# Five dK tiles of a decode backward pass, each stored by two DMAs split along the partitions

## Chip, cores and metric

The kernel runs on one core of a Trainium2 chip. The metric is the device time of one execution in microseconds. The times of before are 742.79, 740.97 and 742.65 us, median 742.65 us.

## What is computed

One token passes through a layer norm and then, side by side, a decode attention block over a cache of 8192 positions (32 heads of 128) and a gated MLP. The reference returns the output and the gradients of all inputs but one:

```python
xn = layernorm(x)
q = (xn @ wq) as 32 heads
p = softmax(q . k_cache * 128 ** -0.5)
out = x + (p . v_cache) @ wo + (silu(xn @ w1) * (xn @ w3)) @ w2
return out, and the gradients of x, k_cache, v_cache, wq, wo, w1, w3, w2 for grad_out
```

All tensors are bf16. `k_cache`, `v_cache` and their gradients dK and dV are 64 MB each (32 heads x 8192 x 128). For one head, dV is the outer product of the probabilities p with the head's gradient `do`, and dK that of the score gradients U with the scaled query `qs`. So the kernel reads some 150 MB and writes as much, and most of it is K, V, dK and dV.

## The kernel before

**Tiles.** A head's 8192 positions lie on 128 partitions, 64 positions on each. A K or V tile is 128 x 64 x 128 bf16, 2 MB, one row of 16 KB on each partition, and this row is contiguous in memory as well. K and V are loaded by SyncE's queue (`load_k` L109, `load_v` L115), three K and two V buffers. dK and dV of a head are built in a tile `ot` of the same shape; the pool has four such buffers.

**Loop.** The main loop runs over the heads. In step h it does the score product of head h+1 (DVE multiplies, L365; TensorE adds up along the head dimension, L367), the softmax, the two attention sums (L429 and L451), and the two outer products of head h. `outer` is called four times in a step: for dV and dK, first and second half. In each half, ScalarE writes 8 of the 32 positions of a partition (L380) and VectorE the other 24 (L387). After the second half (`elif half:` in `outer_v`) the whole tile is stored by one DMA on GpSimd's queue (L394), and up to two pending column stores of a weight gradient follow (L396; these are there around heads 8 and 16 only). The last two heads (`TAIL`) are stored by SyncE's queue in halves (L392).

**What orders the work.** Each engine's instructions run in the order in which they are written. A buffer of `ot` is written again four tiles later, that is dK of head h uses the buffer of dK of head h-2, and its first writers on ScalarE and VectorE wait until the store of that earlier tile has landed. Loads are issued by SyncE as soon as the buffer's last reader is done.

**Queues.** In the profile, q0 is the queue of GpSimd's DMAs (software_dynamic), q1 that of SyncE and q10 that of ScalarE (hardware_dynamic). All of them run on the same 16 DMA engines. At the end of the kernel come the last column stores of wq's and wo's gradients, and the two small outputs, `dx_bf` (128 partitions x 5) by SyncE at L759 and `fin_bf` (5 partitions x 128) by ScalarE at L764.

**Names of the change.** `rows` is the view of `ot` as 128 partitions x 64 positions x 128, `dkc` and `dvc` are dK and dV in memory, seen as head, partition, position, element; `dst` is one of the two.

Of the kernel before, what the change touches and what calls it, by code (L numbers as in the profile page):

```python
# [16 lines left out]
P = 128  # L17
# [4 lines left out]
def kernel(  # L22
# [22 lines left out]
    nc = tc.nc  # L45
# [38 lines left out]
    dkc = out_2.rearrange("b h (p j) d -> (b h) p j d", p=P)  # L84
# [13 lines left out]
    with tc.manual_schedule(engines=ORDERED):  # L98
# [271 lines left out]
        def outer(st, vec, w2, wf, dst, h, half):  # L370
            outer_v(st, vec, w2, dst, h, half, outer_s(st, vec, wf, half))
# [12 lines left out]
        def outer_v(st, vec, w2, dst, h, half, j1):  # L384
            j0 = half * JH
            n = j1 - j0
            nc.vector.tensor_tensor(st.ot[:, j0:j1],  # L387
                                    vec.rearrange("p (a b) -> p a b", b=2).unsqueeze(1).to_broadcast([P, n, DH // 2, 2]),
                                    w2[:, j0:j1, :].unsqueeze(2).to_broadcast([P, n, DH // 2, 2]), ALU.mult)
            rows = st.ot[:].rearrange("p j a b -> p j (a b)")  # L390
            if h >= H - TAIL:
                nc.sync.dma_start(dst[h][:, j0:j0 + JH, :], rows[:, j0:j0 + JH, :])  # L392
            elif half:
                nc.gpsimd.dma_start(dst[h], rows)  # L394
                for _ in range(2 if len(columns) > 2 else len(columns)):
                    nc.gpsimd.dma_start(*columns.pop(0))  # L396

        columns = []

        def row_max(st):  # L400
            st.S = small.tile([P, J], F32, name="S_sb", bufs=1)
            nc.vector.tensor_reduce(st.S[:], st.ps["S"][:], AX.X, ALU.add)  # L402
            mrow = small.tile([P, 1], F32, name="mrow")
            nc.vector.tensor_reduce(mrow[:], st.S[:], AX.X, ALU.max)  # L404
            st.sm = ps_s.tile([P, 512], F32, name="sm", tag="sm")
            nc.tensor.matmul(st.sm[:, 8:8 + P], lhsT=mrow[:].to_broadcast([P, P]), rhs=ident_f[:], start=True, stop=True,  # L406
                             skip_group_check=True)
# [387 lines left out]
```

## Time and profile before

| | |
|---|---|
| time of the profiled execution | 739.76 us |
| its span, first to last instruction | 737.9 us |
| granted TensorE clock, mean | 0.774 |
| data moved | 303.69 MB, mean 412 GB/s |
| HBM read, written | 151.34 MB, 151.34 MB |
| stores of `ot` by GpSimd's queue (L394) | 60, of 2048 KB, landing after 30.5 us (median) |
| shortest and longest landing of an `ot` store | 15.2 us, 40.3 us |
| loads of K and V | 32 and 32, landing after 26.7 and 21.5 us (median) |
| idle time of DVE at L387 for an `ot` store to land | 28.2 us in 14 waits |
| idle time of DVE at L365 for a K load | 29.1 us in 16 waits |

A landing time runs from the issue of a DMA to the arrival of its last byte, queueing included. In the rows of the page, the busy share is that of the span; in the rows of stages, the columns are the stage, its length, the busy time of PE, PEld, DVE, ACT and POOL with the number of instructions, the granted clock, the mean busy share of the 16 DMA engines, and GB/s. In the chain in order of time, each row is a start, a length, and what ran or was waited for.

### The profile page before, as it was taken

Reading aid. Unit: us, or ns where it says so; the run is one execution under the profiler, and the core shown is the slowest. Engines: PE = TensorE matmul, PEld = TensorE weight load, DVE = VectorE, ACT = ScalarE, POOL = GpSimd, SP = SyncE. Lnnn points to the kernel's source line nnn. Section 1 sums busy time; section 2 is a strip of 40 time slices with the busy share of each in tenths; the row PEclk is TensorE's granted clock in tenths of the full one; section 3 lists DMA queues with packets and bytes.
Section 4 is the critical chain, followed back from the end, with each engine's and each line's share of the span. In section 5 each row is a group of like instructions: output and inputs, shape, how many; then the busy total and the mean of one; then the engine's idle time right before and its main releaser. Section 6 shows DMA issues by size and latency. Waiting matters only on the chain.

```text
span 737.9 us, 15773 instructions
## 1 busy us (share of the span) xinstructions
PE 560.1 (76%) x6498; PEld 326.3 (44%) x6513; DVE 628.8 (85%) x708; ACT 467.3 (63%) x1395; POOL 48.6 (7%) x93
## 2 busy tenths in 40 slices
PE   4768888786888788767788877787878767887860
PEld 3554445443544445434444434444444434454440
DVE  3689999997899989877998979699599988999990
ACT  2384566784678666674677656587377846777650
POOL 0010000000000110100000100100000000000100
PEclk9798779767777779667986788688678878867765
DMA  9998999999999999999999999999999999999992
GB/s 332 415 410 311 407 432 428 428 428 429 428 429 429 422 432 426 430 425 427 432 428 426 431 428 425 428 428 426 427 422 410 428 422 432 409 430 430 419 407 106
DMA packets 28389, 303.69 MB, mean 412 GB/s; under 512 B 3116, under 2 KB 4846, under 8 KB 10910
## 3 DMA queue, kind: packets, MB, share of 16 engines
q1 hardware_dynamic: 15202, 155.41, 50.6%
q0 software_dynamic: 11376, 139.42, 44.6%
q10 hardware_dynamic: 1740, 7.87, 2.6%
q8 instruction: 51, 0.84, 0.4%
q14 instruction: 20, 0.16, 0.1%
HBM read 151.34 MB, written 151.34 MB: 410 GB/s over the span
## 4 chain that ended last, share of the span: by engine, by line
DMA 60%; DVE 23%; PE 10%; ACT 3%; issue 1%; SPq 1%; DVEq 0%; ACTq 0%
DMA out_dram<-ot 33%; DMA Kt<-in_A_k_cache_dram 23%; DVE T L365 10%; DVE ot L387 8%; PE psS L367 3%; DMA out_dram<-wo_g 2%; DMA w3t<-in_B_w_dram 2%; ACT ot L380 2%; PE ob L451 1%; PE ob L429 1%; PE psDP L367 1%; DVE DP_sb L436 1%; SPq L158 1%; PE dx_ps L592 1%; DVE S_sb L402 1%
## 5 line engine op out<-in xcount | busy, mean ns | idle before, releaser
L367 PE MATMUL psDP<-T,ident_bf 128*128 128x512 bf16 x512 | 187.7, 533 | 58.0 <-DVE T L365 57.8
L367 PEld LDWEIGHTS <-ident_bf 128*128 128x128 bf16 x1024 | 123.8, 123 | 238.6 <-issue 191.1
L380 ACT ACTIVATE ot<-qs_g,Uf 128x128 bf16<-128x128 bf16 x496 | 151.5, 390 | 60.4 <-DMA out_dram<-ot 18.3
L365 DVE TENSOR_TENSOR T<-Kt,qs_g 128x4096 bf16<-128x4096 bf16 x64 | 146.4, 2289 | 30.6 <-DMA Kt<-in_A_k_cache_dram 29.1
L367 PE MATMUL psS<-T,ident_bf 128*128 128x512 bf16 x512 | 152.2, 451 | 21.6 <-DVE T L365 21.4
L380 ACT ACTIVATE ot<-do_g,Pf 128x128 bf16<-128x128 bf16 x504 | 154.0, 389 | 5.4 <-DMA out_dram<-ot 4.4
L365 DVE TENSOR_TENSOR T<-Vt,do_g 128x4096 bf16<-128x4096 bf16 x64 | 146.1, 2282 | 0.7 <-ACT do_g L284 0.6
L387 DVE TENSOR_TENSOR ot<-qs_g,U 128x3072 bf16<-128x3072 bf16 (+1 forms) x64 | 113.2, 1769 | 23.8 <-DMA out_dram<-ot 23.8
L387 DVE TENSOR_TENSOR ot<-do_g,P 128x3072 bf16<-128x3072 bf16 (+1 forms) x64 | 112.9, 1763 | 5.5 <-DMA out_dram<-ot 4.4
L394 POOL DMA_DIRECT2D out_dram<-ot x60 | 32.1, 535 | 583.0 <-DVE Uf L449 315.9
L451 PEld LDWEIGHTS <-Kt 128*128 128x128 bf16 x2048 | 57.7, 98 | 11.0 <-issue 8.2
L451 PE MATMUL ob<-U,Kt 128*128 128x1 bf16 x2048 | 57.1, 164 | 1.7 <-DVE U L444 1.5
L429 PEld LDWEIGHTS <-Vt 128*128 128x128 bf16 x2048 | 56.8, 98 | 0.0
L429 PE MATMUL ob<-P,Vt 128*128 128x1 bf16 x2048 | 56.1, 163 | 0.0
L423 ACT ACTIVATE Pf<-E,rZ 128x16 f32<-128x16 f32 x32 | 9.7, 305 | 59.8 <-DVE rZ L419 59.8
L470 ACT ACTIVATE dq_diag<-ident_bf,odq 128x128 bf16<-128x128 bf16 x32 | 12.8, 401 | 48.2 <-DVE odq L466 48.2
L406 PE MATMUL sm<-ident_f,mrow 128*128 128x128 f32 x64 | 18.6, 380 | 22.6 <-DVE mrow L404 22.4
L258 ACT COPY woT<-ps_t 128x512 bf16<-128x512 bf16 x40 | 23.0, 577 | 20.0 <-PE ps_t L253 20.0
L440 PE MATMUL sm<-rdot,ones_fc 128*128 128x1 f32 x64 | 11.3, 246 | 21.6 <-DVE junk L439 21.5
L253 PE MATMUL ps_t<-ident_bf,wo_g 128*128 128x128 bf16 x160 | 18.3, 247 | 10.2 <-ACT woT L258 6.7
L440 PEld LDWEIGHTS sm<-rdot,ones_fc 128*128 128x128 f32 x64 | 10.5, 191 | 34.3 <-DVE junk L439 32.2
L402 DVE TENSOR_REDUCE S_sb<-psS 128x64 f32<-128x512 f32 x32 | 21.9, 685 | 3.1 <-PE psS L367 3.1
(154 smaller groups left out, 501.6 us busy)
## 6 DMA issues: line engine op xcount, KB each, us to landing
out_dram<-ot POOLq DMA_DIRECT2D x60, 2048.0 KB, 30.5
Kt<-in_A_k_cache_dram SPq DMA_DIRECT2D x32, 2048.0 KB, 26.7
Vt<-in_A_v_cache_dram SPq DMA_DIRECT2D x32, 2048.0 KB, 21.5
out_dram<-ot SPq DMA_DIRECT2D x8, 1024.0 KB, 16.5
out_dram<-wo_g ACTq DMA_DIRECT2D x6, 640.0 KB, 15.5
wo_g<-in_A_wo_dram ACTq DMA_DIRECT2D x6, 640.0 KB, 15.8
wq<-in_A_wq_dram SPq DMA_DIRECT2D x2, 1280.0 KB, 27.8
out_dram<-wq POOLq DMA_DIRECT2D x10, 256.0 KB, 35.0
```

The costliest lines, as they stand in the source:

```text
L253: nc.tensor.transpose(ps_t[:, hh * DH:(hh + 1) * DH], wo_g[:, hh, ci * P:(ci + 1) * P], ident_bf[:])
L258: nc.scalar.copy(woT[:], ps_t[:])
L365: nc.vector.tensor_tensor(T[:], src[:, :, ds_], vec[:, ds_].unsqueeze(1).to_broadcast([P, J, DHH]), ALU.mult)
L367: nc.tensor.matmul(ps[:], lhsT=ident_bf[:], rhs=T[:, :, RUN * i:RUN * (i + 1)], start=(half == 0 and i == 0), stop=(half == 1 and i == DHH ...
L380: nc.scalar.activation(st.ot[:, j1 - ACT_J + j].rearrange("p a b -> p (a b)"), vec, ACTF.Copy, scale=wf[:, half, j:j + 1])
L387: nc.vector.tensor_tensor(st.ot[:, j0:j1], vec.rearrange("p (a b) -> p a b", b=2).unsqueeze(1).to_broadcast([P, n, DH // 2, 2]), w2[:, j0: ...
L394: nc.gpsimd.dma_start(dst[h], rows)
L402: nc.vector.tensor_reduce(st.S[:], st.ps["S"][:], AX.X, ALU.add)
L406: nc.tensor.matmul(st.sm[:, 8:8 + P], lhsT=mrow[:].to_broadcast([P, P]), rhs=ident_f[:], start=True, stop=True, skip_group_check=True)
L429: nc.tensor.matmul(st.ob[:, 0:1], lhsT=st.V[:, j, :], rhs=st.P2[:, j, 0:1], start=(j == 0), stop=(j == J - 1), skip_group_check=True)
L440: nc.tensor.matmul(st.sm[:, 4:5], lhsT=ones_f, rhs=rdot[:], start=True, stop=True, skip_group_check=True)
L451: nc.tensor.matmul(st.ob[:, 1:2], lhsT=st.K[:, j, :], rhs=st.U2[:, j, 0:1], start=(j == 0), stop=(j == J - 1), skip_group_check=True)
```

## The change

For heads 20, 22, 24, 26 and 28, the dK tile's store is cut along the partitions into two DMAs on the same queue, one right behind the other: partitions below 120, 124, 126, 127 and 104, and then the 8, 4, 2, 1 and 24 that are left. dV tiles and the dK tiles of all other heads are stored as before, and nothing is computed in another way.

```diff
             elif half:
-                nc.gpsimd.dma_start(dst[h], rows)
+                cut = CUT.get(h, P) if dst is dkc else P
+                nc.gpsimd.dma_start(dst[h][0:cut], rows[0:cut])
+                if cut < P:
+                    nc.gpsimd.dma_start(dst[h][cut:P], rows[cut:P])
                 for _ in range(2 if len(columns) > 2 else len(columns)):
                     nc.gpsimd.dma_start(*columns.pop(0))

         columns = []
+        CUT = {20: 120, 22: 124, 24: 126, 26: 127, 28: 104}
```

On the engines this adds five DMA issues to GpSimd's 93 instructions. The one that stores a single partition is issued as 16 runs of 512 elements. The later writers of these five buffers wait for the completion of both DMAs. The order of the instructions on each engine stays as it was.

## The prediction

> **What bounds the kernel now.** I read the page first (busy rows, slices, DMA queues, chain), then the stages, the chain in order of time, and last the DMA view of the final 98 us.
>
> ```profile
> span 737.9 us, 15773 instructions
> ...
> PE 560.1 (76%) x6498; PEld 326.3 (44%) x6513; DVE 628.8 (85%) x708; ACT 467.3 (63%) x1395; POOL 48.6 (7%) x93
> ...
> q0 software_dynamic: 11376, 139.42, 44.6%
> q10 hardware_dynamic: 1740, 7.87, 2.6%
> ...
> DMA 60%; DVE 23%; PE 10%; ACT 3%; issue 1%; SPq 1%; DVEq 0%; ACTq 0%
> ```
>
> The longest share of the chain is DMA. The stages say that this is throughput and not latency: from 380 us to 680 us the 16 DMA engines are busy all the time (share 1.00 or more).
>
> ```profile
> 380.00:480.00 100.00, 78.47 (x853) 44.11 (x854) 85.44 (x92) 64.19 (x197) 9.15 (x17) 0.74 1.01 428
> 480.00:580.00 100.00, 78.96 (x953) 45.24 (x952) 87.77 (x96) 68.92 (x214) 4.83 (x9) 0.77 1.00 423
> 580.00:680.00 100.00, 78.00 (x940) 45.96 (x940) 89.39 (x98) 69.00 (x211) 5.34 (x10) 0.79 1.01 425
> 680.00:738.00 58.00, 28.57 (x373) 17.19 (x373) 38.43 (x55) 23.65 (x74) 3.63 (x5) 0.66 0.76 315
> ```
>
> The chain there is store, outer product, store: a dK tile's store lands, DVE may write that buffer again two heads later, and so on.
>
> ```profile
> 603.93 33.76 DMA out_dram<-ot
> ...
> 637.71 1.76 DVE ot L387
> ...
> 644.74 33.01 DMA out_dram<-ot
> ...
> 677.77 1.76 DVE ot L387
> ```
>
> From 677.77 us the chain is DVE work to about 718 us, and then one thing more holds the end: SyncE's last wait, 16.2 us on the 1.2 KB store of `dx_bf`. The DMA view from 640 us to the end shows why (40 slices of 2.45 us):
>
> ```profile
> DMA  9999999999999999999999999999999999200000
> GB/s 354 401 428 441 428 428 428 415 428 435 441 428 428 421 441 428 428 421 435 428 428 398 413 420 410 440 409 395 376 406 420 416 404 362 96 23 27 27 27 0
> ```
>
> 429 GB/s over 16 engines is 26.8 GB/s for one. In the last slices 23, 27, 27, 27 GB/s move: one engine drains alone for four slices, 9.8 us, while 15 idle. That engine is late, its backlog sets the end, and what is added to its work in the last third is paid in full.
>
> The price of a row follows: 16,384 bytes at 26.8 GB/s are 0.611 us on one engine, and a whole tile is 128 rows, 8 for each engine, 4.9 us.
>
> **The change, part by part.** (1) Issue. Five GpSimd DMAs become ten. One issue takes 535 ns (POOL, L394, x60, 32.1 us), so +2.7 us on an engine that is 7% busy. Behind the second issue on POOL stands only the next head's dV store, which comes 8 to 12 us later (573.13, 581.32, 593.20 in POOL's timeline); the extra column DMAs of L396 all lie at earlier heads. Each second issue also waits for the store issued eight before it on this queue: some 80 us old at one store in 10 us, while the longest landing is 40.3 us. Cost 0. SP's order does not move, nor ACT's or PE's.
>
> (2) Release. The next writers of the buffer (ACT L380, DVE L387) wait for two semaphores, two heads later: one more 21 ns wait instruction on DVE and on ACT for most of the five tiles, below 0.2 us in all.
>
> (3) Bytes: none added. The second pieces' completions are 16 writes of 4 bytes each.
>
> (4) Which engine moves which row. This is the edit. No software-queue transfer of before has a row count that 16 does not divide, so the distribution is bounded. I take shares of ceil(rows/16), filled from the front. Then 120, 124, 126 and 127 rows put 8 on each engine until they run out, as now, and the engines at the end get 8, 4, 2 and 1 fewer; 104 rows put 7 on each and none on the last. The pieces of 8, 4 and 2 rows add one row to as many front engines, the 24 rows add two; the single row is issued as 16 runs of 1 KB, below 0.1 us on each. So an engine carries between 4 rows more (the first two: +1, +1, +1, 2-1) and 23 fewer (the last: 8+4+2+1+8). In time: +2.4 us to -14.1 us. Only the late engine's share counts, because the 15 others have 9.8 us to spare.
>
> Where does the late engine stand? The trace's records of single packets show that in its lonely stretch it also moved one of the five rows of `fin_bf`, a store of five partitions. In queue q10's row, 1740 packets are 12 `wo_g` transfers at 128 rows and 16 completions (1728), 1 row of `g_row`, 5 of `fin_bf`, and 6 more: one completion for an engine that took part, 1 and 5. So five rows went to five engines and the late one is among them. If those are the front five, its extra is 4, 4, 3, 3 or 2 rows, mean 3.2: **+2.0 us**. I take this. [...]
>
> (5) Speed of a row in a split tile. Whole tiles run at 0.611 us a row. Below: no difference, 0. Above: the rows reach the engines in another order, two engines want the same path, and each row takes twice as long: 8 x 0.611 = 4.9 us a tile, 24.4 us for five. The nearest row is L583, a store of 64 of the 128 partitions (80 KB, landed after 7.5 us, against 7.9 us for the 160 KB one issued just before): no doubling shows, though the queue ahead hides most of it. I take 0 and keep 24.4 for the range.
>
> **Sum.** 0 + 0.2 + 2.0 + 0: +2 us. The profiled run took 739.76 us (span 737.9 and 1.9 us around it), 2.9 us below the median of 742.65; the same 2 us on the median give **744.6 us**. Since 0.3% (2.2 us) is about what a measurement of this kernel can tell from no change, the forecast itself lies at that border. Its own range is 742 to 747.
>
> **Rivals.**
>
> *Two engines on one path.* As (5): up to +24.4 us on the late engine. For: it runs behind the others, so it would read a split tile while they read whole ones, and stores are about half of all packets (q0 44.6% against q1 50.6%), so it would meet another's store half of the time: 5 x 8 x 0.3 = +12 us, 757 us with the extra rows, between 746 and 769. Against: L583. [...] Chance 0.20.
>
> *Few engines.* q10 shows that five rows used five engines and one row one. If the software queue also wants a number of engines that divides the rows, 127 is prime and goes to one engine: 119 rows more than now, 72.7 us; 124 goes to four, 31 rows each, +23 rows, 14.1 us. An engine that is not the late one has 9.8 us to spare: +63 us; if both fall on the late one, +87. I price +73: 816 us. DVE at 85 to 89% cannot make that up. For: q10. Against: q0's 11376 packets divide by 16 (711), so each software-queue issue, small ones included, left a completion on all 16. [...] Chance 0.13.
>
> *Relief: faster.* The late engine is the one that serves the top rows. Then the pieces take up to 23 rows off it, 14.1 us, of which 9.8 us can be won before the other 15 set the end: 732.9 us. It decides only where the late engine is the sixteenth in order; the ninth to the fifteenth get between 1 row more and 2 fewer. For: the alone stretch is real and reaches the end. Against: that engine served `fin_bf`, a five-row store. Chance 0.07.
>
> *No effect.* The front engines are not the late one and all extra rows hide in the 9.8 us: 742.7 us. Chance 0.03.
>
> **Chances and range.** Forecast 0.57, of which 0.31 within 0.3% and 0.26 above, as 4 rows or a few slower ones pass 2.2 us and 2 or 3 do not. Slower 0.26 + 0.20 + 0.13 = 0.59; same 0.31 + 0.03 = 0.34; faster 0.07. The range leaves out the few-engine case and relief, 0.20 together: low 740.5 (the forecast at no cost, at the low end of the times shown), high 766 (742.65 + 2 + most of the 24.4).
>
> **What would show it.** Right: dK stores of split heads land a microsecond or two later, GB/s of 480 to 680 us stays at 420 or more, the lonely 27 GB/s stretch at the end grows from 9.8 us to about 12, q0 has 95 packets more (five times 16 completions, and 16 runs for the single row). Two engines on one path: landings of split tiles some 5 us longer and the lonely stretch 15 to 25 us. Few engines: a stretch near 625 us (dK of head 26) with GB/s far below 400 and landings above 70 us. Relief: the lonely stretch is gone. I am wrong in the mechanism if the time moves while that stretch stays as long as it is.

## The result, and the profile after

The changed kernel takes 749.06 us (median of 8 runs, 746.08 to 752.36), the kernel before 740.75 us beside it (8 runs, 738.75 to 742.79). The ratio is 1.0111, interval 1.0083 to 1.0139: slower by 8.3 us, between 6.1 and 10.3. The forecast was 744.6 us. The time lies inside the range and on the side that was forecast, but above the 742 to 747 that the forecast gave itself.

The profiled execution took 746.08 us, the shortest of the eight, so its profile shows 6.3 of the 8.3 us (span 744.2 against 737.9). Its page, in the rows that answer to those of before:

```profile
span 744.2 us, 15783 instructions
...
PE 549.7 (74%) x6498; PEld 320.4 (43%) x6513; DVE 629.4 (85%) x708; ACT 467.6 (63%) x1395; POOL 51.2 (7%) x98
...
q0 software_dynamic: 11536, 139.42, 44.8%
...
DMA 54%; DVE 26%; PE 13%; ACT 2%; issue 1%; SPq 1%; DVEq 0%; ACTq 0%
```

The busy times of DVE (628.8 before) and ACT (467.3) have not moved: no engine has more to do. The megabytes of q0 are the same too. Its packets are 160 more, where 95 were forecast; that difference is taken up below.

The stages show where the time went (stage, length, busy time of PE, PEld, DVE, ACT and POOL, granted clock, DMA share, GB/s):

```profile
480.00:580.00 100.00, 75.80 (x943) 43.76 (x944) 83.47 (x92) 64.43 (x200) 5.90 (x11) 0.76 1.00 410
580.00:680.00 100.00, 76.89 (x882) 43.98 (x881) 91.13 (x98) 71.10 (x217) 6.43 (x12) 0.77 1.00 410
680.00:744.00 64.00, 33.28 (x443) 19.88 (x441) 41.33 (x59) 25.82 (x81) 4.19 (x6) 0.63 0.81 330
```

In both stages that hold the split tiles, the DMA engines are still busy all the time (1.00), but they move 410 GB/s where they moved 423 and 425. That is 13 + 15 = 28 GB/s over 100 us each, 2.8 MB less by 680 us, and 2.8 MB at 425 GB/s are 6.6 us. The span has grown by 6.3 us. So the loss is complete before the end begins: busy engines that move less.

The end has not become longer. The DMA view from 640 us to 745 us, 40 slices of 2.6 us (mean busy tenths of the engines, GB/s):

```profile
DMA  7999999999999999999999999999999999511100
GB/s 321 338 308 350 424 437 431 425 424 437 424 437 431 412 443 406 399 406 387 406 437 409 389 407 415 422 416 409 405 415 414 424 399 382 197 70 51 54 26 3
```

Before, one engine drained alone through four slices at 23 to 27 GB/s. Now there are slices of 70, 51 and 54 GB/s, two engines and more, and one of 26, one engine alone. The stretch of few engines still lasts about four slices, but 51 and 54 GB/s are two engines at 26.8 each: a second engine has fallen behind. The section on single rows comes back to it.

The split tiles themselves land hardly later. The issues of GpSimd's queue in small windows around each of the five (us from issue to landing, at the right), first after:

```profile
out_dram<-ot POOLq DMA_DIRECT2D x1, 1920.0 KB, 39.6
out_dram<-ot POOLq DMA_DIRECT2D x1, 128.0 KB, 40.9
...
out_dram<-ot POOLq DMA_DIRECT2D x1, 1664.0 KB, 31.1
out_dram<-ot POOLq DMA_DIRECT2D x1, 384.0 KB, 32.2
...
out_dram<-ot POOLq DMA_DIRECT2D x1, 2032.0 KB, 30.2
```

and before, the tiles of heads 20, 28 and 26 in that order:

```profile
out_dram<-ot POOLq DMA_DIRECT2D x1, 2048.0 KB, 38.7
...
out_dram<-ot POOLq DMA_DIRECT2D x1, 2048.0 KB, 30.8
...
out_dram<-ot POOLq DMA_DIRECT2D x1, 2048.0 KB, 32.9
```

Tiles 20 and 28 land 2.2 and 1.4 us later than whole ones did. Tile 26, cut at 127, lands no later (its last row, stored by the second DMA, after 31.0 us), and tiles 22 and 24 take 33.6 and 36.7 us against 33.0 and 36.5. What moves is when the next tile is stored. The chain in order of time after (start, length, what):

```profile
496.64 40.87 DMA out_dram<-ot
...
545.16 33.57 DMA out_dram<-ot
...
586.39 36.68 DMA out_dram<-ot
...
669.36 32.17 DMA out_dram<-ot
```

These are the second pieces of heads 20, 22, 24 and 28, so four of the five split tiles now stand on the chain. In POOL's timelines the store of the same heads began at 495.54, 541.25, 581.32, 624.84 (head 26) and 664.79 us before, and the second piece now starts at 496.64, 545.16, 586.39, 630.66 and 669.36: 1.1, 3.9, 5.1, 5.8 and 4.6 us later, of which half a microsecond is the first piece's issue. The delay builds up tile by tile over heads 20 to 24 and stays.

### The profile page after: what moved, and what is told of

Its sections match the earlier page's. It is cut to its first block, busy times and chain, and to the rows that moved or that the text cites. A ratio compares the mean times of both kernels' runs of the same rounds, so it can differ in the third digit from the quotient of the medians.

```text
span 744.2 us, 15783 instructions
## 1 busy us (share of the span) xinstructions
PE 549.7 (74%) x6498; PEld 320.4 (43%) x6513; DVE 629.4 (85%) x708; ACT 467.6 (63%) x1395; POOL 51.2 (7%) x98
## 3 DMA queue, kind: packets, MB, share of 16 engines
q0 software_dynamic: 11536, 139.42, 44.8%
## 4 chain that ended last, share of the span: by engine, by line
DMA 54%; DVE 26%; PE 13%; ACT 2%; issue 1%; SPq 1%; DVEq 0%; ACTq 0%
DMA Kt<-in_A_k_cache_dram 27%; DMA out_dram<-ot 25%; DVE T L365 12%; DVE ot L387 9%; PE psS L367 4%; PE ob L433 2%; DMA w3t<-in_B_w_dram 2%; PE psDP L367 2%; PE ob L455 2%; DVE S_sb L406 1%; DVE DP_sb L440 1%; SPq L158 1%; PE dx_ps L596 1%; ACT ot L380 1%; DVE T L593 1%
## 5 line engine op out<-in xcount | busy, mean ns | idle before, releaser
L367 PE MATMUL psDP<-T,ident_bf 128*128 128x512 bf16 x512 | 183.7, 524 | 61.2 <-DVE T L365 61.2
L367 PEld LDWEIGHTS <-ident_bf 128*128 128x128 bf16 x1024 | 121.4, 121 | 241.8 <-issue 191.7
L380 ACT ACTIVATE ot<-qs_g,Uf 128x128 bf16<-128x128 bf16 x496 | 151.5, 390 | 70.4 <-DMA out_dram<-ot 26.8
L367 PE MATMUL psS<-T,ident_bf 128*128 128x512 bf16 x512 | 148.5, 443 | 25.1 <-DVE T L365 25.1
L455 PEld LDWEIGHTS <-Kt 128*128 128x128 bf16 x2048 | 57.5, 98 | 10.3 <-issue 7.6
L410 PEld LDWEIGHTS sm<-ident_f,mrow 128*128 128x128 f32 x64 | 11.1, 218 | 33.2 <-DVE mrow L408 31.7
```

Of the source, the lines that this page charges most:

```text
L367: nc.tensor.matmul(ps[:], lhsT=ident_bf[:], rhs=T[:, :, RUN * i:RUN * (i + 1)], start=(half == 0 and i == 0), stop=(half == 1 and i == DHH ...
L380: nc.scalar.activation(st.ot[:, j1 - ACT_J + j].rearrange("p a b -> p (a b)"), vec, ACTF.Copy, scale=wf[:, half, j:j + 1])
L455: nc.tensor.matmul(st.ob[:, 1:2], lhsT=st.K[:, j, :], rhs=st.U2[:, j, 0:1], start=(j == 0), stop=(j == J - 1), skip_group_check=True)
```

## The experiments

The reading above leaves three suspects: the extra rows on the late engine (term 4 of the prediction), the speed of rows in a split tile (term 5), and the second DMA as such. Twelve kernels take them apart. Every ratio is against the kernel before, timed on the same chip beside it. In the diffs, lines that do not change are left out, and so is the table `CUT` where it only lists the five heads; `...` marks a gap between changed lines.

### Two DMAs a tile, cut along the positions

All 128 partitions take part in both DMAs; only the row is cut, 8 KB and 8 KB.

```diff
-                nc.gpsimd.dma_start(dst[h], rows)
+                if dst is dkc and h in CUT:
+                    nc.gpsimd.dma_start(dst[h][:, 0:JH, :], rows[:, 0:JH, :])
+                    nc.gpsimd.dma_start(dst[h][:, JH:J, :], rows[:, JH:J, :])
+                else:
+                    nc.gpsimd.dma_start(dst[h], rows)
```

> The same five dK tiles are stored by two DMAs each, but cut along the positions: both DMAs take all 128 partitions, 8 KB of each row. Theory 'extra rows' (some engines get more rows, the late one pays): no engine gets more bytes, +0 us. Theory 'path' (with a row count other than 128 the rows go to the engines in another order and two engines read over one path): the order is that of a whole tile, +0 us. Theory 'two DMAs' (a second issue and a second completion cost the time by themselves): the loss of the changed kernel, +8 us, ratio 1.011.

Measured: 741.30 us against 740.38, ratio 1.0013 (1.0000 to 1.0025), +0.9 us. Five more issues, their completions and the second wait of the next writers cost 2 us by the upper end of the interval at most. The second DMA as such is not the 8.3 us.

### All five cut at 127, and all five at 120

With equal shares filled from the front, which is the author's assumption, a cut at 127 leaves the engines as many rows as a whole tile but for the last one; a cut at 120 puts a row more on eight front engines each time (8 from the first piece, 1 from the second).

```diff
-        CUT = {20: 120, 22: 124, 24: 126, 26: 127, 28: 104}
+        CUT = {h: 127 for h in range(20, 29, 2)}
```

> All five tiles are cut at partition 127, so that the second DMA stores one partition in 16 runs of 1 KB. 'Extra rows': the front engines keep 8 rows, nothing is added to the late one, +0 us (below 0.5). 'Path': five tiles whose 127 rows go to the engines in order, +8 us or more, bounded by 5 x 4.9 = 24 us; GB/s between 480 and 680 us stays at 410 as in the changed kernel. 'Two DMAs': +8 us.

> All five tiles are cut at partition 120 (120 and 8 rows). 'Extra rows': each of the first eight engines gets one row more per tile, 5 x 0.61 = +3.1 us and nothing else. 'Path': as with 127, +8 us or more; if both theories hold, some 3 us above the kernel cut at 127. 'Two DMAs': +8 us.

Measured: 745.01 us for 127, ratio 1.0063 (1.0044 to 1.0081), +4.6 us; 750.02 us for 120, ratio 1.0126 (1.0111 to 1.0141), +9.6 us. The stages of the kernel cut at 127:

```profile
480.00:580.00 100.00, 74.79 (x950) 43.20 (x948) 84.33 (x93) 65.26 (x202) 5.90 (x11) 0.81 1.00 413
580.00:680.00 100.00, 76.06 (x879) 43.14 (x880) 91.14 (x99) 70.61 (x215) 6.35 (x12) 0.81 1.00 412
```

413 and 412 GB/s with all engines busy: the rate falls although, by these shares, no engine received a 16 KB row more. Five tiles cut at 127 cost 4.6 us, 0.9 us a tile (0.7 to 1.2). So the cut itself has a price, and the piece of 8 rows, or the place of the cut, costs as much again.

### The extra rows alone

Here the five tiles are stored whole, and a second DMA stores their last 8 rows once more, into scratch memory. Nothing is cut, but eight engines get a row more: q0 has 160 packets more (11,536 against 11,376), for each piece 8 rows and 24 writes below 512 bytes, which are 16 completions and 8 that make up 16 equal shares. In the sister kernel it is the last 4 rows, on four engines by the same shares.

```diff
                 nc.gpsimd.dma_start(dst[h], rows)
+                if dst is dkc and h in CUT:
+                    spare = nc.dram_tensor(f"spare_{h}", (8, J, DH), BF16, kind="Internal").ap()
+                    nc.gpsimd.dma_start(spare, rows[120:P])
```

> The five dK tiles are stored whole, by one DMA as before, and a second DMA behind each stores the last 8 rows once more, to a scratch buffer in memory (0.64 MB more in all, 1.5 us of all engines at 429 GB/s). It keeps the usual row order and adds only the second piece of the cut at 120. 'Extra rows': the first eight engines get one row more for each tile, five in all: +3.1 us, and with the cut at 127 (+4.6 us, order alone) it makes up most of the +9.6 us of the cut at 120. 'Path alone': the order is unchanged, so below +1.5 us, and the cut at 120 costs more than 127 for a reason of its order.

> As the kernel that stores the last 8 rows of the five whole tiles once more, but with the last 4 rows only. In the changed kernel's records the late engine took a row of the 8-row piece and none of the 4-row piece, so it is one of the fifth to the eighth. Theory 'only the late engine's share counts': four engines that are not late get the row more, and the time grows only by what a second DMA costs, +0.5 to +1.5 us (0.9 us with the cut along the positions), against +4.5 us with 8 rows. Theory 'any engine's extra row counts' (no engine has time to spare): five rows more on four engines, +3 to +4.5 us as with 8.

Measured: with 8 rows 744.53 us against 740.06, ratio 1.0054 (1.0038 to 1.0070), +4.5 us; with 4 rows 740.45 us against 740.74, ratio 0.9996 (0.9986 to 1.0007), nothing. The stages, first with 8 rows, then with 4:

```profile
480.00:580.00 100.00, 76.96 (x949) 44.75 (x947) 84.52 (x93) 65.28 (x203) 5.88 (x11) 0.77 1.00 419
580.00:680.00 100.00, 76.23 (x877) 43.95 (x878) 89.51 (x97) 70.05 (x214) 6.35 (x12) 0.77 1.00 416
```

```profile
480.00:580.00 100.00, 79.14 (x924) 44.85 (x923) 85.95 (x94) 66.22 (x207) 5.89 (x11) 0.76 1.00 421
580.00:680.00 100.00, 80.91 (x963) 46.86 (x960) 90.48 (x98) 69.63 (x212) 6.91 (x13) 0.78 1.00 421
```

A piece of a sixteenth of a tile (128 KB behind 2 MB), five times, costs 4.5 us, and half of it costs nothing. The bytes cannot do that: five pieces of 128 KB are 0.66 MB, 1.5 us at 425 GB/s if all 16 engines were short of time. Five rows on one engine are 5 x 0.611 = 3.1 us, and the interval of 2.8 to 5.2 us holds it. So one engine's share decides, and if small pieces fill the engines from the front, as assumed, it is one of the fifth to the eighth: touched by 8 rows, not by 4. The late engine of the prediction is confirmed in kind; its lag, given below with the single rows, shows it directly.

The DMA view of the kernel with 8 rows, its last 103 us (slices of 2.6 us), shows that the lonely stretch does not take the added rows up:

```profile
GB/s 286 299 324 369 445 426 420 426 445 420 426 420 445 420 426 426 439 433 426 420 426 445 387 420 426 420 425 425 385 407 417 409 407 388 128 22 25 29 25 0
```

22, 25, 29 and 25 GB/s: four slices, 10.3 us, against 9.8 us before. 3 us were added to the engine that is alone there, and the stretch is as long as it was within a slice. The loss stands in the middle, as a rate of 419 and 416. I read it so: the `ot` buffers come free only when a tile's last row has landed, so the other engines can run only so far ahead, and from there on a delay of the late engine makes them move less. No run tests this reading by itself; a kernel with more `ot` buffers would.

### More ways to cut

> All five tiles are cut at partition 64 (64 and 64 rows, four for each engine in each DMA). 'Extra rows': none, +0 us. [...] 'Two DMAs': +8 us. If this one costs nothing and the one cut at 127 costs 8, row counts that 16 divides keep an order without conflicts.

Cut in the middle, 64 and 64 (4 rows an engine and piece, 8 in all): 746.00 us, ratio 1.0082 (1.0059 to 1.0105), +5.6 us (4.4 to 7.8). By equal shares no engine has a row more, and the price is that of 127 (3.3 to 6.0) within the intervals.

> All five tiles are cut at 112 (112 and 16 rows, 7 and 1 for each engine: no engine gets a row more). [...] If the loss comes with any order but that of a whole tile (or from the order in which the rows reach the main memory), +4.6 us as with 127. 'Two DMAs' alone: +0.9 us, as with the cut along the positions.

Cut at 112 and 16 (7 rows and 1, again 8 in all; q0 has 80 packets more, the completions alone): 750.88 us against 740.62, ratio 1.0132 (1.0116 to 1.0148), +10.3 us. This is twice the price of 127, and twice the +4.6 us that the expectation gave to any order but that of a whole tile; no extra row explains it.

> The dK tiles of heads 1 to 29 (29 tiles) are cut at 127. 'Path': five tiles cost 4.6 us, 0.9 us for each, so 29 cost 27 us, about 767 us, and GB/s falls below 420 in every stage from 80 us on. If the loss lies only with where the five tiles stand (a queue that runs dry once), it stays below +10 us.

The dK tiles of heads 1 to 29, all cut at 127 (29 tiles): 798.73 us, ratio 1.0774 (1.0732 to 1.0817), +58.7 us, 2.0 us a tile. Its stage moves 368 GB/s:

```profile
480.00:580.00 100.00, 70.13 (x766) 39.46 (x766) 74.44 (x81) 56.84 (x176) 8.03 (x15) 0.70 0.97 368
```

The cost is there and far larger than any extra row (none is added), but the price per tile is not constant: 0.9 us for five tiles, 2.0 us for 29. A linear price was wrong. The loss builds up along the run: from 80 to 180 us the rate is still 421 GB/s (429 before), from 280 us on it is 383, 380, 368 and 386 in the stages of 100 us.

### Rows one by one

The trace keeps the packets one by one, without the name of the engine that moved them. A 16 KB row of a store on GpSimd's queue takes 0.611 us in the median; before, 7,126 of the 7,680 rows took just that. The number of those rows that took over 0.700 us, and the time over 0.611 us of all those rows together:

| kernel | slow rows | excess, us | us lost by the timing |
|---|---|---|---|
| before | 102 | 32 | 0 |
| last 4 rows twice | 100 | 34 | 0 |
| last 8 rows twice | 111 | 34 | 4.5 |
| all five cut at 127 | 217 | 102 | 4.6 |
| all five cut at 120 | 237 | 112 | 9.6 |
| all five cut at 64 | 221 | 112 | 5.6 |
| all five cut at 112 | 193 | 98 | 10.3 |
| the change | 209 | 100 | 8.3 |
| 29 tiles cut at 127 | 1012 | 585 | 58.7 |

The two terms can be told apart here. Extra rows alone leave the rows as fast as they were (111 slow ones). Cut tiles double the number. If all that the cut at 127 adds lies in the five tiles, 69 us in 640 rows, a row of them takes 0.72 us in the mean. Spread over 16 engines, 69 us would be 4.3 us on each, which is the size of the 4.6 us; but they are not spread evenly, as the next table shows. Nor does the excess follow the price: of the cuts of five tiles, the one at 112 costs most and has the least. It slows the loads too: 301 rows of 16 KB on SyncE's queue took over 0.700 us, against 204 before and 245 with the cut at 127. That is a lead for its higher price and no explanation.

Of each store, the trace also keeps the 16 completions, read here as one from each engine. For the `ot` stores on GpSimd's queue that landed between 520 and 680 us, the median time by which the last completion comes after the second-last, and the second-last after the third-last:

| kernel | last engine behind, us | second-last behind, us |
|---|---|---|
| before | 12.5 | 1.1 |
| last 4 rows twice | 12.7 | 1.0 |
| last 8 rows twice | 15.9 | 0.7 |
| all five cut at 127 | 5.1 | 5.4 |
| all five cut at 120 | 8.0 | 5.9 |
| all five cut at 64 | 15.5 | 0.4 |
| all five cut at 112 | 14.6 | 1.0 |
| the change | 6.9 | 6.0 |

Before, one engine is late by 12.5 us. With 8 rows stored again it is late by 3.4 us more, about the five rows (3.1 us); with 4 rows by no more. So the extra rows do sit on the late engine, and its lead can grow in the middle of the run. The cuts do something else: with 127, 120 and the change, a second engine falls behind, and in the stores of the change that land after 680 us it is 10.8 us behind the third-last and the last one only 0.4 us behind it. Cut at 64 or 112, the late engine alone falls further back.

Why a row in a split tile is slower, on the side of SBUF or of memory, was not settled. Nor was why the loss falls on one engine or on two, or how it turns into the time lost.

### Whose queue: the stores on SyncE and on ScalarE

The rival of few engines says that 127 rows go to one engine. On GpSimd's queue, nothing of the kind appears: the 2032 KB piece above landed after 30.2 us, while 127 rows on one engine would take 127 x 0.611 = 77.6 us. To see whether it appears on another queue, all stores were put on SyncE's, whole, and then the tile of head 26 was cut there.

```diff
-                nc.gpsimd.dma_start(dst[h], rows)
+                cut = CUT.get(h, P) if dst is dkc else P
+                nc.sync.dma_start(dst[h][0:cut], rows[0:cut])
+                if cut < P:
+                    nc.sync.dma_start(dst[h][cut:P], rows[cut:P])
...
+        CUT = {26: 127}
```

> All 60 whole-tile stores go out on SyncE's queue instead of GpSimd's; nothing is cut. If the late engine is late because of the software queue's stores, its lonely stretch at the end (9.8 us at 27 GB/s) goes away and up to 9.8 us are won, 731 us; against that, loads now stand behind stores on SyncE, whose waits for the last VectorE write of a tile can hold back a K load: 0 to 3 us a head in the worst case. Otherwise, if the late engine is late by itself, no change beyond that loss.

> As the kernel with all stores on SyncE's queue, with one more change: the dK tile of head 26 is cut at 127. 'Few engines' (the hardware queue takes a number of engines that divides the rows; 127 is prime): one engine moves 127 rows, 119 more than its share: 119 x 0.611 = +73 us over that kernel, less up to 10 us if that engine was not the late one, so +60 to +75 us, a stretch of some 60 us at the rate of few engines near 640 us, and that store lands 80 us or more after its issue. Otherwise (rows shared as on the software queue): +1 us.

Measured: whole, 747.53 us, ratio 1.0098 (1.0081 to 1.0115), +7.5 us; with one tile cut at 127, 816.97 us, ratio 1.1035 (1.1004 to 1.1066), 69.4 us more than whole. The DMA view of the second from 600 us to 816 us, slices of 5.4 us, and then two rows of SyncE's timeline (start, length, what):

```profile
DMA  9999999410000099498820000199999996765991
GB/s 426 420 434 410 437 416 394 185 49 30 27 27 27 27 337 352 140 382 349 306 109 27 24 27 27 76 376 343 415 426 433 425 428 278 323 278 229 413 375 29
```

```profile
634.28 0.27 SPq L395 DMA_DIRECT2D out_dram<-ot  x1
634.60 37.71 SPq L397 DMA_DIRECT2D out_dram<-ot  x1
```

After the store of the 127 rows was issued at 634.28 us, the chip moves 27 GB/s, one engine's rate, from 649 to 676 us and again from 713 to 735 us; between, the other engines work. SyncE itself stands for 37.71 us at the next issue, and the loads behind it on the queue wait: the next one, of K, is issued at 672.41 us. The queue's packets tell it too: SyncE's queue had 23,842 of them with whole stores and has 23,828 now, 14 fewer. A whole tile is 128 rows and 16 completions, 144; 127 rows with one completion and one row with one are 130. So on the hardware queue 127 rows went to one engine.

The two queues treated the same 127 rows differently: on SyncE's one engine moved them, at +69.4 us, and on GpSimd's there was no such stretch. Why, and what other numbers of rows would do, these runs do not show.

With all stores on SyncE's queue, whole, the end looks different. The DMA view of the kernel with all stores on SyncE's queue from 640 us to the end:

```profile
GB/s 431 406 437 406 399 350 418 331 462 418 399 462 393 325 331 359 425 438 403 471 423 428 412 431 437 424 328 225 403 353 212 262 150 393 412 399 406 340 45 3
```

No lonely stretch: the rate goes from 340 to 45 to 3. A late engine is not gone, though: between 520 and 680 us the last of the 16 completions of a transfer on this queue still comes 5 to 7 us after the second-last. The kernel is slower; the drops to 212 and 150 GB/s fit stores and loads that wait for each other on one queue. If the stretch is lost time, a queue with fewer such drops should win. ScalarE's queue was tried, first for the dV stores, then for dV and dK (the diff is that of both).

```diff
-                nc.gpsimd.dma_start(dst[h], rows)
+                if dst is dvc:
+                    st.rows_dv = rows
+                else:
+                    st.rows_dk = rows
...
+                nc.scalar.dma_start(dkc[prev.h], prev.rows_dk)
...
+                nc.scalar.dma_start(dvc[h], c.rows_dv)
```

> Nothing is cut. The 30 dV stores go out on ScalarE's queue, issued after ScalarE's share of the next half tile; the 30 dK stores stay on GpSimd's queue. With all stores on a hardware queue the lonely stretch at the end was gone, but SyncE's loads stood behind stores. Theory 'late engine': half of the late engine's slow rows go, 3 to 5 us are won, about 736 us. Theory 'issue': each dV store starts some 4 us later, the buffers come back later, and the time is the same or up to 5 us longer.

> As the kernel before it, and the dK stores go out on ScalarE's queue as well, some 4 us later than now. 'Late engine': no slow rows are left, the lonely stretch goes, 6 to 9.8 us are won, 731 to 734 us. 'Issue': the buffers come back later for all tiles, +0 to +10 us.

Measured: dV alone 747.86 us, ratio 1.0102 (1.0076 to 1.0129), +7.2 us; both 742.91 us, ratio 1.0029 (1.0019 to 1.0040), +2.3 us. Neither beats the kernel before. With both, the DMA view from 640 us to 745 us ends in slices of 191, 29, 7, 12 and 0 GB/s (2.6 us each): a slice at about one engine's rate, and two below it. That the lonely stretch is worth having away is not shown: no version in this study is faster.

## Why the prediction came out as it did

The time lies in the stated range and on the forecast side, but the forecast mechanism does not carry it. Against the kernel before beside it, 740.75 us, 2 us were forecast and 8.3 measured. 749.06 us is outside the forecast's own 742 to 747 and inside the 746 to 769 of *Two engines on one path*, which had a chance of 0.20. The range held because it had been widened for that rival.

**The bound.** Right. The engines stay busy at 1.00 and the rate alone falls, by 2.8 MB up to 680 us, and this is the whole of the span's growth.

**Steps 1 to 3 (issue, release, bytes): 0.2 us.** Right within what can be measured: the cut along positions, with the same five extra DMAs, costs 0.9 us (0 to 1.9), and the five extra DMAs of 4 rows nothing.

**Step 4 (extra rows on the late engine): 2.0 us.** Right in kind. Equal shares of ceil(rows/16) are shown by an odd count. q0 has 160 packets more: 80 are the five completions of 16, 15 are the single row's 16 runs in place of one, and 65 are further writes of 4 bytes (q0 has 1,489 of 4 bytes, 1,344 before). They are just what pads each piece to 16 equal shares: 8, 4, 2, 1 and 8 for the pieces of 120, 124, 126, 127 and 104 rows, and 8, 12, 14 and 8 for those of 8, 4, 2 and 24. The same count gives the 160 packets more of the five tiles cut at 127, cut at 120 or with 8 rows stored again, and the 928 of the 29 tiles cut at 127 (32 a tile). That the shares fill from the front, no count shows; it stays the author's assumption. Nor does any run show what the 2.0 us rest on, that the five rows of `fin_bf` went to the front five engines and the late one is among these, at a mean of 3.2 rows. With shares filled from the front, the pair of 8 and 4 extra rows puts it among the fifth to the eighth, where only two tiles add a row: head 20's, and head 28's (7 + 2 instead of 8). Two rows are 1.2 us by the row's own time; by the 4.5 us of five rows they would be 1.8.

**Step 5 (speed of a row in a split tile): 0, bounds 0 and 24.4 us.** This is the term that failed, by its size. It was put at 0 by the nearest row, the store of 64 partitions at L583, though the text said that the queue ahead hides most of what that row can show. The runs give 4.6 us (3.3 to 6.0) for five tiles cut at 127 and 5.6 us for five cut at 64. Slower rows, which were a rival's effect, are at work, at a fifth of its upper bound. The doubled time of a row behind that bound is not shown (0.72 us in the mean against 0.611, if all the excess lies in the five tiles), nor that two engines meet on one path: the cut at 112 costs 10.3 us with 193 slow rows, the one at 127 4.6 us with 217. Their place is not only the late engine, as the rival had it: a second engine falls behind.

**The sum, made again.** Extra rows 1.2 to 1.8 and a cut's price of 4.6 to 5.6, which holds the five extra DMAs already: 6 to 7 us, against 8.3 measured (6.1 to 10.3). The five tiles cut at 120 fit such a sum: 4.6 for the cut and 4.5 for the 8-row pieces, 9.1 against 9.6 measured. They do not prove it, since the cut at 112 costs 10.3 us, 2.1 us a tile, with no row more on any engine: the place of the cut can double the price by itself. For the pieces of 120, 124, 126 and 104 rows the price without extra rows was not measured, so the split of the 8.3 us between the two terms stays open.

**Few engines.** Refuted for this queue, by the landing of 30.2 us and by the padding; shown on the hardware queue for 127 rows, at +69.4 us, where the working had priced +63 for a tile that misses the late engine. That the number of engines has to divide the rows is not shown beyond that.

**Relief and no effect.** Neither. By shares filled from the front, the pieces took up to 23 rows off the last engine, and nothing came of it: by these shares it is not the late one.

**The sign to look for.** The prediction said that the lonely stretch would grow from 9.8 to 12 us, and that the mechanism is wrong if the time moves while it does not. The time moved and the stretch did not grow, so by its own sign the mechanism was wrong. What failed is the step from "its backlog sets the end" to "so added work shows at the end". The other engines were taken to have 9.8 us to spare. Five more rows on the late engine cost 4.5 us and left the stretch as long as it was; the price is paid in the middle, where the rate fell to 410 against the 420 or more of the other sign. That the four `ot` buffers hold the others back, each waiting for the last of 16 engines, is the likely reason, and not tested.

## What to carry to other kernels

Where DMA sets the pace and buffers are handed back on a transfer's last byte, look for the one of the 16 engines that is late and count the rows that an edit puts on it: here five of them cost 4.5 us, and the cost stood in the rate of the middle, not in the tail. Keep large stores whole over the partitions; if one has to be cut, cut along the row (0.9 us for five tiles) rather than along the partitions (4.6 to 10.3 us). On the software queue 127 rows still went to all 16 engines (landed after 30.2 us, one write of padding); on SyncE's hardware queue they went to one (+69 us for one 2 MB store).

## What was not expected of the hardware

- In the change, the software queue filled unequal pieces up to 16 equal shares with writes of 4 bytes: 65 of them, counted exactly.
- One engine of 16 falls behind along the run before: a transfer's last completion on GpSimd's queue comes 1.1 us after the second-last (median) between 100 and 300 us, 4.5 us between 300 and 480, and 14.8 us from 680 us on. With all stores on SyncE's queue the lonely stretch is gone, but one engine is still 5 to 7 us behind, so the lateness does not belong to the software queue's stores alone. Which engine it is stays in part open: it moved a row of the five-row store `fin_bf`, and the pieces of 8 and 4 rows put it between the fifth and the eighth, so the fifth fits both only if both kinds of queue fill from the front and count from the same engine, which no run shows.
- Five tiles cut at 127 or 120 make a second engine late, and it stays late to the end.
- Cutting 29 tiles costs 2.0 us a tile where five cost 0.9, and a cut at 112 costs 2.1 us a tile where 127 costs 0.9. Both stay open.
